# The second product of attention takes both operands in two parts for the first two pairs of heads too

## The chip, the cores and the metric

One core of a Trainium2 chip runs the whole program in one launch. The engines that matter are TensorE (PE in the profile; PEld is its weight load), VectorE (DVE), ScalarE (ACT), GpSimd (POOL) and SyncE (SP), whose queue issues every DMA. Each engine works through its own instructions in a fixed order. The metric is device microseconds of one execution, and three runs of the kernel before are given.

## The reference

Three blocks are chained, all in float32. Only the first is touched by the change; the other two follow it in the same program.

```python
def _attn_ref(q, k, v, g_q, g_k):          # q, k, v: (4, 12, 448, 64)
    q_n, k_n = rmsnorm(q, g_q), rmsnorm(k, g_k)
    scores = scale * q_n @ k_n^T
    attn = exp(scores - max) ; attn = attn / (sum + 1e-9)
    return attn @ v                          # the second product
...
x = attn_out as (1792, 768)
h = ((x @ w1) * (x @ w2)) @ w3 @ w_out      # first block of weights, d_ff 1024
g = h2 * clip(h2 + 3, 0, 6) / 6, h2 = h @ w_in ; out = g @ w_out2   # second, d_ff 2048
```

## The kernel before, in words

**Work and stages.** The 48 heads are taken as 24 pairs (index `i`), both heads of a pair at once. A pair is eight *steps* of scores: `score` (lines 627 and 628, two matmuls), `scale_max` on VectorE (634), `expo` on ScalarE (646). Eight steps later the same pair's probabilities come back through TensorE: `trans` (653) transposes them in seven blocks `kb` of 128 keys, four small matmuls each, into a PSUM bank of the tag "t", of which there are two. `thi` (662, ScalarE) copies a block from the bank to SBUF as `xh`. One step on, `tlo` (672, VectorE) would subtract it from the bank to give the rest, `xl`. Two steps on, `pv` multiplies the block with `v`. Blocks 0 to 2 and 4 to 6 belong to one head each; block 3 holds 64 keys of either head, and its two products run on separate halves of the array.

**Two forms of the second product.** `full(i)` is true for pairs 0 and 1. There `v` is loaded straight into `vo`, `xh` is plain float32, there is no `xl`, and a block's product is one float32 matmul (line 701, and line 687 for block 3), which the hardware runs as two instructions. For all other pairs `v` is loaded into `vr`, of which there is one buffer, and `vsplit` makes two parts of it: ScalarE rounds it (615), GpSimd subtracts (616). The parts stand side by side as 128 columns. A block then takes two matmuls in the reduced format float32r, one for `xh` (705, or 693 in block 3) and one for `xl` (706, or 693 again). Both leave two halves of the result in 128 rows of PSUM, so `xcopy` (713) moves one half and `xadd` (721, VectorE) adds the other.

**What runs between.** A stream of matmuls that doesn't depend on attention fills TensorE: first `wprime` (line 252, plain float32, 128 products, w3 times w_out), later layers 1 and 2. Their weights come from HBM as 64-bit numbers into four `raw` buffers and are converted by ScalarE (148, 149) and VectorE (151). `fill` hands out a fixed amount of this stream to every step. `at(t, ...)` and `SHIFT` put the small tasks into steps. A scheduler with its own model of time then orders the instructions of each engine. In the instruction stream of the first two pairs and what runs beside them, all of this is mixed closely.

```python
def full(i):
    return i in FULL                                  # 471
...
hi = ap.tile([P, S], F32 if full(i) else F32R, tag="xh", bufs=3, name="xh")   # 655
...
if full(i):                                           # 700
    nc.tensor.matmul(T["pv", i, j][:64, :S], vo[:, j, kb % 4], hi, ...)
    return
w = vo[:, j, kb % 4].rearrange("p a d -> p (a d)")
nc.tensor.matmul(ps, w, hi, start=(kb == 0), stop=False)
nc.tensor.matmul(ps, w, lo, start=False, stop=(kb == 6))
```

Of the kernel before, what the change touches and what calls it, by code (L numbers as in the profile page):

```python
# [36 lines left out]
NH = DM // 2  # L37
XB = 7
TAGS = ("s", "t", "v", "f")
FULL = (0, 1)  # L40
LG = 8
AHEAD = 3
K3 = 12
# [7 lines left out]
def fused_kernel(ctx: ExitStack, tc: tile.TileContext, nat, qT, kT, vin, gq, gk,  # L51
# [418 lines left out]
    def attention(ap, rate):  # L470
        def full(i):
            return i in FULL

# [945 lines left out]
```

## Time and profile before

| | |
|---|---|
| median of 3 runs | 1149.24 us (1142.69, 1149.24, 1151.27) |
| the profiled execution | 1141.81 us, span of its instructions 1140.0 us |
| TensorE busy | 1103.1 us, 97% of the span |
| weight loads | 944.0 us, 83% |
| VectorE, ScalarE, GpSimd busy | 850.8 (75%), 812.4 (71%), 177.9 (16%) us |
| DMA | 299.04 MB, 262 GB/s on average |

Averages hide that the stages differ: attention with `wprime` beside it fills roughly the first 190 us, attention with the next layers runs on to about 620 us, and the rest is matrix products alone. The plain float32 products of pairs 0 and 1 stand between 41.9 and 94.7 us. A busy TensorE isn't a TensorE at its peak, because the ends of pipelined matmuls are modelled; the distance from one start to the next is the better measure of what a matmul costs in a dense stretch.

### The profile page before, as it was taken

How to read it: one execution, taken by the hardware profiler on the slowest of the kernel's cores; microseconds unless marked ns; L12 is line 12 of the kernel's file. 1: busy time of each engine (PE TensorE's matmuls, PEld its weight loads, DVE VectorE, ACT ScalarE, POOL GpSimd, SP SyncE). 2: the span in 40 equal slices, each digit the busy share in tenths (PEclk: the TensorE clock that was granted, in tenths of full speed). 3: DMA queues.
4: the chain of work that ended last, by engine and by line, in shares of the span. 5: the costliest groups of instructions: out<-in, count | busy, mean ns of one | idle time of the engine just before them, and what ended most of it. 6: DMA issues, size and time to landing. Idle time of an engine off the chain costs nothing.

```text
span 1140.0 us, 17361 instructions
## 1 busy us (share of the span) xinstructions
PE 1103.1 (97%) x5483; PEld 944.0 (83%) x5483; DVE 850.8 (75%) x1927; ACT 812.4 (71%) x1729; POOL 177.9 (16%) x156
## 2 busy tenths in 40 slices
PE   5999999999999999999999999999999999999998
PEld 3545666788887888888888899899989989999998
DVE  5757988779866888778753225999988998887764
ACT  6989778899758878787754433766666776666764
POOL 1133223554322213221102000000000000000000
PEclk9999999999999999999999999999999999999999
DMA  8999655689889988997789998665469955434972
GB/s 267 331 317 342 213 171 164 243 293 377 272 279 316 308 295 269 336 342 253 232 287 324 382 362 299 217 214 200 164 228 362 389 172 168 153 117 160 335 264 74
DMA packets 109660, 299.04 MB, mean 262 GB/s; under 512 B 13280, under 2 KB 46048, under 8 KB 109568
## 3 DMA queue, kind: packets, MB, share of 16 engines
q1 hardware_dynamic: 109568, 297.93, 76.2%
q8 instruction: 43, 0.70, 0.3%
q14 instruction: 49, 0.40, 0.1%
HBM read 230.61 MB, written 67.27 MB: 261 GB/s over the span
## 4 chain that ended last, share of the span: by engine, by line
PE 60%; ACT 7%; DMA 7%; DVE 3%; issue 2%; POOL 0%; SPq 0%; ACTq 0%; POOLq 0%; DVEq 0%
PE acc L1304 17%; PE bank L391 10%; PE sB L1242 8%; PE sA L1242 8%; PE bank L396 5%; DMA rsb<-rsd 2%; PE bank L653 2%; ACT PP L646 1%; PE bank L88 1%; PE bank L89 1%; PE bank L90 1%; PE bank L627 1%; PE bank L628 1%; PE bank L706 1%; DMA raw<-in_wo_dram 1%
## 5 line engine op out<-in xcount | busy, mean ns | idle before, releaser
L1304 PE MATMUL acc<-g,wt 128*128 128x448 f32 x1008 | 211.7, 366 | 1.2 <-ACT g L1192 1.0
L1304 PEld LDWEIGHTS acc<-g,wt 128*128 128x128 f32 x1008 | 188.9, 188 | 17.7 <-ACT g L1192 1.9
L391 PE MATMUL bank<-xhl,ws 128*128 128x448 f32 x768 | 180.5, 367 | 1.6 <-ACT bs L367 1.3
L391 PEld LDWEIGHTS bank<-xhl,ws 128*128 128x128 f32 x768 | 143.5, 188 | 15.1 <-ACT bs L367 1.8
L634 DVE CUSTOM_DVE_ANT_0 PP<-bank,rb,rq 112x448 f32<-112x448 f32 x192 | 128.7, 675 | 27.4 <-PE bank L628 21.1
L646 ACT ACTIVATE PP<-PP,mx 112x448 f32<-112x448 f32 x192 | 127.5, 665 | 28.1 <-DVE mx L641 24.3
L1242 PE MATMUL sA<-xo,wt 128*128 128x448 f32 x504 | 112.0, 366 | 1.1 <-ACT u L1253 1.1
L1242 PE MATMUL sB<-xo,wt 128*128 128x448 f32 x504 | 112.2, 367 | 0.8 <-ACT u L1253 0.6
L252 PE MATMUL bank<-woh,w 128*128 128x384 f32 x256 | 97.6, 509 | 14.6 <-DVE woh L151 10.9
L1242 PEld LDWEIGHTS sB<-xo,wt 128*128 128x128 f32 x504 | 94.4, 188 | 9.9 <-ACT u L1253 1.9
L1242 PEld LDWEIGHTS sA<-xo,wt 128*128 128x128 f32 x504 | 94.6, 188 | 9.6 <-ACT u L1253 1.5
L662 ACT ACTIVATE xh<-bank 128x448 fp32r<-128x448 f32 (+1 forms) x156 | 83.1, 539 | 24.6 <-PE bank L653 20.5
L653 PEld LDWEIGHTS bank<-ident,PP 112*128 112x128 f32 x672 | 78.8, 141 | 23.9 <-issue 6.1
L1011 DVE TENSOR_TENSOR wt<-wf,wt 128x384 fp32r<-128x384 f32 x160 | 87.3, 555 | 15.1 <-ACT wt L1010 14.9
L672 DVE TENSOR_TENSOR xl<-bank,xh 128x448 fp32r<-128x448 f32 x142 | 87.4, 617 | 11.5 <-ACT xh L662 10.1
L653 PE MATMUL bank<-ident,PP 112*128 112x112 f32 x672 | 94.1, 261 | 1.5 <-DVE xl L672 1.1
L396 PE MATMUL bank<-xhl,ws 128*128 128x448 f32 x384 | 94.5, 366 | 0.0
L252 PEld LDWEIGHTS bank<-woh,w 128*128 128x128 f32 x256 | 48.9, 196 | 43.7 <-DVE woh L151 13.4
L148 ACT ACTIVATE raw<-raw 128x384 f32<-128x384 f32 (+1 forms) x112 | 63.8, 569 | 28.6 <-DMA raw<-in_wo_dram 11.6
L1010 ACT ACTIVATE wt<-wf 128x384 fp32r<-128x384 f32 x160 | 80.4, 517 | 4.8 <-PE acc L1304 2.7
L151 DVE SCALAR_TENSOR_TENSOR raw<-raw 128x384 int32<-128x384 int32 x80 | 48.9, 613 | 46.0 <-ACT raw L149 38.8
L627 PE MATMUL bank<-K,Q 128*112 128x448 f32 x192 | 77.7, 407 | 1.5 <-DVE mx L634 1.4
(134 smaller groups left out, 2110.3 us busy)
## 6 DMA issues: line engine op xcount, KB each, us to landing
ws<-w12d SPq DMA_DIRECT2D x48, 768.0 KB, 6.2
ws<-wpd SPq DMA_DIRECT2D x32, 768.0 KB, 6.5
wf<-wfd SPq DMA_DIRECT2D x56, 384.0 KB, 5.6
raw<-in_wo_dram SPq DMA_DIRECT2D x44, 384.0 KB, 5.8
td<-G SPq DMA_DIRECT2D x32, 448.0 KB, 2.5
G<-td SPq DMA_DIRECT2D x32, 448.0 KB, 6.2
raw<-in_w_dram SPq DMA_DIRECT2D x32, 384.0 KB, 6.9
w12d<-ws SPq DMA_DIRECT2D x16, 768.0 KB, 5.9
```

The lines of the kernel that those rows point to most:

```text
L252: nc.tensor.matmul(ps[:, :NH], W["w3"][a, c // 4][:, cs], W["woh"][c, n], start=c == 0, stop=c == M1 - 1)
L391: nc.tensor.matmul(ps[:, :S], w[:, 0, ks], x[:, y, :], start=k == 0 and y == 0, stop=False)
L396: nc.tensor.matmul(ps[:, :S], w[:, 1, ks], L["xhl"][i][:, 0, :], start=False, stop=k == KD - 1)
L627: nc.tensor.matmul(ps[:CP, :S], qs, k1[:, j, :], start=True, stop=False)
L634: anchors[8 * i + s].append(nc.vector.tensor_tensor_reduce(out=T["PP", i][:, c, sl], in0=ps[:CP, :S], in1=T["rb", i][:, sl], op0=ALU.mult, ...
L646: anchors[8 * i + s].append(nc.scalar.activation(v, v, AF.Exp, bias=T["m", i][:, 8 + s : 9 + s], accum_out=T["sum", i][:, s : s + 1]))
L653: nc.tensor.transpose(ps[:, c * CP : c * CP + CP], src[:, c, kb * P : kb * P + P], ident[:CP, :CP])
L662: nc.scalar.activation(hi, ps, AF.Copy)
L672: nc.vector.tensor_sub(lo, ps, hi)
L1011: nc.vector.tensor_sub(t[:, 1, :], src, t[:, 0, :])
L1242: mm = nc.tensor.matmul(ps[:, :S], w[:, a, ks], x[:, c, :], start=first and k == 0 and n == 0, stop=k == KD // 2 - 1 and n == 2, skip_grou ...
L1304: nc.tensor.matmul(ps, w[:, y, ns], x[:, z, :], start=first and a == 0, stop=end and a == 2, skip_group_check=h in "674")
```

## The change

The tuple of pairs that take the plain float32 form becomes empty. Pairs 0 and 1 then go through `vsplit`, `tlo`, the two reduced-format matmuls a block and `xadd`, as the other 22 pairs do.

```diff
-FULL = (0, 1)
+FULL = ()
```

Counted over the program: 12 matmuls of line 701 and 4 of line 687 go; 12 of line 705, 12 of line 706 and 8 of line 693 come. VectorE gets 14 subtractions of line 672 and 4 additions of line 721, ScalarE 2 copies of line 615, GpSimd 2 subtractions of line 616. The number of DMAs is the same; two loads of `v` go to `vr` and not to `vo`.

The scheduler orders the instructions anew. On TensorE the two orders are alike up to the 66th matmul and again for the last 3,706 of some 5,330. The first place is TensorE's order where the first block of pair 0 meets `v` (`K,Q`: scores, `ident,PP`: transposes, `xh,vo` and `xl,vo`: second product, `woh,w`: the `wprime` stream). Before:

```order
L653 MATMUL bank<-ident,PP 128x112 x4
L701 MATMUL bank<-xh,vo 64x448
L627 MATMUL bank<-K,Q 112x448
L628 MATMUL bank<-K,Q 112x448
L653 MATMUL bank<-ident,PP 128x112 x4
L701 MATMUL bank<-xh,vo 64x448
```

and now:

```order
L653 MATMUL bank<-ident,PP 128x112 x8
L627 MATMUL bank<-K,Q 112x448
L628 MATMUL bank<-K,Q 112x448
L252 MATMUL bank<-woh,w_107 128x384 x4
L705 MATMUL bank<-xh,vo 128x448
L706 MATMUL bank<-xl,vo 128x448
L705 MATMUL bank<-xh,vo 128x448
L706 MATMUL bank<-xl,vo 128x448
```

Both first blocks are now transposed before any product; two more scores stand ahead of the transposes, and four matmuls of the other stream stand between them and the first product.

The second place is SP's order of DMAs at the loads of `v` for the first pairs (`raw`: weights, `qr`, `kr`, `rb`: operands of later pairs). Before:

```order
L99 DMA nat<-in_nat_dram 112x1024
L99 DMA vo<-in_v_dram 128x512 x2
L99 DMA rb<-rkd 112x896
L99 DMA qr<-in_qT_dram 128x896
L99 DMA kr<-in_kT_dram 128x896
L99 DMA vr<-in_v_dram 128x512
```

and now, from the same DMA on:

```order
L99 DMA nat<-in_nat_dram 112x1024
L99 DMA vr<-in_v_dram 128x512
L99 DMA rb<-rkd 112x896
L99 DMA qr<-in_qT_dram 128x896
L99 DMA kr<-in_kT_dram 128x896
L99 DMA raw<-in_wo_dram 128x768 x3
L99 DMA wpd<-wst 128x256
L99 DMA raw<-in_wo_dram 128x768
L99 DMA wpd<-wst 128x256 x5
L99 DMA vr<-in_v_dram 128x512
L99 DMA qr<-in_qT_dram 128x896
L99 DMA raw<-in_w3t_dram 128x1024
```

One load of `v` stands ahead of the weights where three stood. The second now waits until GpSimd has split the first, because `vr` has one buffer, and a load of w3 stands behind it.

## Rows read from the trace of the kernel before

**Rows 1.** The page: busy tenths in 40 slices of 28.5 us.
```profile
PE   5999999999999999999999999999999999999998
PEclk9999999999999999999999999999999999999999
```

**Rows 2.** Busy time by stretch; the last three columns are granted clock, DMA share, GB/s.
```profile
core 0: us, PE busy (x) PEld busy (x) DVE busy (x) ACT busy (x) POOL busy (x), PEclk, DMA share, GB/s
40.00:60.00 20.00, 19.33 (x75) 10.58 (x75) 13.14 (x41) 20.00 (x45) 4.20 (x4) 1.00 1.04 332
60.00:80.00 20.00, 18.50 (x67) 9.78 (x66) 9.99 (x24) 15.29 (x34) 4.56 (x5) 1.00 1.01 319
80.00:100.00 20.00, 20.00 (x79) 10.92 (x78) 12.70 (x39) 19.12 (x42) 7.36 (x7) 1.00 0.98 345
100.00:120.00 20.00, 18.70 (x84) 12.62 (x83) 16.53 (x40) 19.56 (x45) 7.63 (x7) 1.00 0.93 321
120.00:140.00 20.00, 19.12 (x89) 12.57 (x88) 18.97 (x52) 15.36 (x36) 5.66 (x5) 1.00 0.69 216
...
620.00:1140.00 520.00, 512.21 (x2508) 469.81 (x2506) 385.14 (x722) 317.15 (x638) 2.29 (x2) 1.00 0.67 238
```

**Rows 3.** What PE waited for, 40 to 100 us: in total, times, longest.
```profile
PE bank L252 <- DVE wst L245: 1.5, 1, 1.5
PE bank L701 <- DMA vo<-in_v_dram: 0.5, 1, 0.5
```

**Rows 4.** The same, 100 to 140 us.
```profile
PE bank L705 <- ACT xh L662: 1.3, 1, 1.3
PE bank L706 <- DVE mx L641: 0.6, 1, 0.6
PE bank L653 <- DVE xl L672: 0.2, 1, 0.2
```

**Rows 5.** PE in order of time: start, us, line, count; plain float32 products and followers.
```profile
43.78 0.97 PE L701 MATMUL bank<-xh,vo 128*64 128x448 f32 x2
44.67 0.46 PE L627 MATMUL bank<-K,Q 128*112 128x448 f32 x1
44.97 0.37 PE L628 MATMUL bank<-K,Q 128*112 128x448 f32 x1
45.17 5.32 PE L252 MATMUL bank<-woh,w 128*128 128x384 f32 x16
...
53.08 0.97 PE L687 MATMUL bank<-xh,vo 64*64 64x448 f32 x4
53.98 0.46 PE L627 MATMUL bank<-K,Q 128*112 128x448 f32 x1
```

**Rows 6.** The same, products in two parts of pairs 2 and 3, and followers.
```profile
102.60 0.45 PE L706 MATMUL bank<-xl,vo 128*128 128x448 f32 x1
102.89 0.36 PE L705 MATMUL bank<-xh,vo 128*128 128x448 f32 x1
103.09 0.55 PE L653 MATMUL bank<-ident,PP 112*128 112x112 f32 x4
...
107.91 0.47 PE L705 MATMUL bank<-xh,vo 128*128 128x448 f32 x1 [1.30 <-ACT xh L662]
108.22 0.37 PE L627 MATMUL bank<-K,Q 128*112 128x448 f32 x1
...
115.67 0.66 PE L705 MATMUL bank<-xh,vo 128*128 128x448 f32 x1
116.17 0.55 PE L653 MATMUL bank<-ident,PP 112*128 112x112 f32 x4
...
133.31 0.47 PE L693 MATMUL bank<-xh,vo 64*128 64x448 f32 x2
133.72 0.46 PE L627 MATMUL bank<-K,Q 128*112 128x448 f32 x1
...
135.99 0.47 PE L693 MATMUL bank<-xl,vo 64*128 64x448 f32 x2
136.39 0.47 PE L705 MATMUL bank<-xh,vo 128*128 128x448 f32 x1
```

**Rows 7.** Instructions on tiles vr and xl: ns min/median/max, first and last start.
```profile
L615 ACT ACTIVATE vo<-vr x2: 622/630/637, 69.8 to 98.4; 128x512 fp32r<-128x512 f32 x2
L616 POOL TENSOR_TENSOR vo<-vr,vo x2: 1276/1401/1526, 70.9 to 99.1; 128x512 fp32r<-128x512 f32 x2
...
L672 DVE TENSOR_TENSOR xl<-bank,xh x13: 574/616/625, 101.1 to 137.1; 128x448 fp32r<-128x448 f32 x13
```

**Rows 8.** ACT by line, 40 to 100 us: busy, mean ns, idle before.
```profile
L148 ACT ACTIVATE raw<-raw 128x384 f32<-128x384 f32 x13 | 7.5, 580 | 3.7 <-DMA raw<-in_w_dram 3.7
L148 ACT ACTIVATE raw<-raw 128x512 f32<-128x512 f32 x8 | 5.4, 680 | 1.2 <-DMA raw<-in_w3t_dram 1.2
```

**Rows 9.** DVE by line, 38 to 140 us.
```profile
L721 DVE TENSOR_TENSOR xs<-bank,xs 64x448 f32<-64x448 f32 x3 | 1.8, 613 | 0.0
```

**Rows 10.** SP's own waits, 30 to 140 us.
```profile
SPq L99 <- POOL vo L616: 2.5, 2, 2.2
```

**Rows 11.** All matmuls of line 252: ns min/median/max, first and last start in us.
```profile
L252 PE MATMUL bank<-woh,w x256: 483/486/1010, 8.3 to 190.1; 128*128 128x384 f32 x128
```

## The prediction

> **What bounds the kernel now.** I read first the page's slices: from the second one on TensorE is busy at nine tenths or more and its clock is granted in full [rows 1]. Then the table by stretch. It says that from 40 to 100 us, where pairs 0 and 1 have their second product, nearly everything is full at once: TensorE 57.8 of 60 us, ScalarE 54.4, the DMA engines a share of 0.98 to 1.04; only VectorE (35.8) and GpSimd (16.1) have room [rows 2]. After 620 us TensorE is busy 512 of 520 us, so what is gained or lost early is carried to the end: nothing later absorbs it. Third, who kept TensorE waiting: 2.0 us in those 60 us, one wait for an eviction of `wprime` and one for the load of `v` [rows 3]. So TensorE sets the pace there, ScalarE and DMA are just behind it, and a saving on TensorE counts as long as these two keep up. In the next 40 us, where pairs 2 and 3 already go in two parts, TensorE waited 2.1 us [rows 4].
>
> **TensorE, removed.** In a dense stretch a plain float32 product lasts until the next start: 43.78 to 44.67, 0.89 us, and the two products of block 3, which run side by side, 53.08 to 53.98, 0.90 us together [rows 5]. Pairs 0 and 1 have six of the first and one of the second each: 12 x 0.89 + 2 x 0.90 = 12.5 us.
>
> **TensorE, added.** A matmul of a part takes 0.20 us to the next start (102.89 to 103.09), 0.29 to 0.31 (102.60 to 102.89, 107.91 to 108.22), or 0.50 behind a `wprime` matmul whose tail it carries (115.67 to 116.17). Block 3 takes 0.41 for both high parts and 0.40 for both low ones [rows 6]. I take 0.30, the middle of the three, since the new order has all three kinds of neighbours: 24 x 0.30 + 2 x 0.81 = 8.8 us. Saving 3.7 us. With 0.20 throughout it is 6.1; with 0.50 throughout there would be a loss of 1.1. The Trainium skill, "FP8 and Floating Point Precision", TensorE Precision Notes, says that true float32 takes four passes of the array. Two parts are two passes, so by that rule half of the array's time goes: with 0.20 us a pass, as in the shortest row, 14 slots x 0.4 = 5.6 us, and the forecast below would be 1142.7 instead of 1144.6. The rows have the removed side near that rule (0.89 against 0.80), but the added matmuls mostly cost more than a bare pass, so I stay with 3.7.
>
> **VectorE.** 14 subtractions of 0.616 us and 4 additions of 0.613 [rows 7, 9]: 11.1 us, of which 35.8 + 11.1 = 46.9 still fit into 60. The throughput costs nothing; the cover is VectorE's idle 24 us. But each subtraction stands between the copy `xh` and the second matmul of its block, and holds a "t" bank 0.62 us longer than before, so it can become a wait of TensorE. What such waits cost is seen where pairs 2 and 3 have 13 of these subtractions: 2.1 us in all [rows 4, 7]. For 14: 2.3 us. Bounds: nothing, if the new order covers every one; 14 x 0.616 = 8.6 us if every one lies bare. I take 2.3, because it is measured with the same neighbours and an equally full ScalarE (19.56 of 20 [rows 2]).
>
> **ScalarE and GpSimd.** Two more `vsplit`: 2 x 0.63 = 1.3 us on ScalarE, 2 x 1.4 = 2.8 on GpSimd [rows 7]. GpSimd has 44 us of room. ScalarE has none from 40 to 60 (20.00 of 20.00), and 4.7 us from 60 to 80 [rows 2], idle there because it waited for weights [rows 8]. Queued behind the first `vsplit` are the exponentials and the conversions. I cost it at nothing beyond the 2.3, since that stretch, too, had a copy of line 615 just ahead of it, at 98.4 [rows 7]; without the cover it is 1.3.
>
> **The first product and the loads.** Before, TensorE waited 0.5 us for the load of `v` at 41.9 [rows 3]. Now the two copies come behind the same load: 0.63 + 1.4 = 2.0 us later. The order puts in front of that product two more scores (0.5 us each by 44.67 to 45.17) and four `wprime` products, which are eight instructions, half of the sixteen that take about 5 us: 1.0 + 2.6 = 3.6 us [rows 5]. So the delay is covered; uncovered it would be 2.0. On SP's queue one load of `v` instead of three stands ahead of the weights. That is kind to a full DMA stretch. But the second and third load of `vr` now wait for GpSimd, and loads of w3 stand behind them. Such waits took 2.5 us for two [rows 10]. Two more, 2.5 us, are mostly hidden, as transfers issued earlier are still running at a share of 1.0 [rows 2]; I cost them at nothing, 2.5 if the DMA engines ran dry.
>
> **Sum.** -3.7 + 2.3 = -1.4 us. The profiled execution would go from 1141.81 to 1140.4 us (span 1140.0 to 1138.6). It stands 7.4 us below the median of the three runs, as low as the lowest of them. The four executions together have their middle at (1142.69 + 1149.24) / 2 = 1146.0, and I put the forecast on that: 1144.6, rounded 1145 us, which is 4.6 us below the median shown, though only 1.4 of it is the change. Chance 0.5 for a net of about -3 to 0.
>
> **Rival: the parts come late, slower.** The place is pairs 0 and 1, the price the subtractions. ScalarE is full there, so the copies `xh` come late, `xl` later still, and TensorE stands in order behind line 706 or behind a transpose that lacks a bank. Fully bare: -3.7 + 8.6 + 1.3 = +6.2, 1152.2 us. It decides from 3.7 / 14 = 0.26 us bare for each block on. For it: ScalarE 20.00 of 20.00; a wait of 1.3 us for one `xh` in the stretch in two parts [rows 4]. Against it: that stretch shows 0.16 us a block, and the scheduler put other work between. Chance 0.18.
>
> **Rival: the saving is hidden.** DMA share 1.0 says that the weights set the pace of `wprime`, whose matmuls stand in TensorE's fixed order; then a shorter product only becomes a wait for weights: 1146.0. For it: ScalarE's 4.9 us of waits for weights [rows 8]. Against it: TensorE itself waited for none of that [rows 3]. Chance 0.12.
>
> **Rival: ScalarE sets the pace.** Then its added 1.3 us are the whole effect, +1.3, 1147.3 us. For it the full 20 us at the start; against it the idle 4.7 us right after [rows 2]. The Trainium skill, "Perfetto Trace Analysis", Identifying the Most-Contended Engine, judges ScalarE by its busy share and TensorE by its weight loads, and would have ScalarE improved first; weight loads fill 10.58 of the same 20 us. By that rule this change loads the wrong engine. The waits show TensorE as the one that stops for almost nothing, so I give it 0.08.
>
> **Rival: all of it is kept.** Every wait is covered and the short spacing holds: -3.7 to -6.1, 1139.9 to 1142.3. Chance 0.12. That the change doesn't do what it says is excluded by the order: no plain float32 second product is left.
>
> **How the numbers follow.** The range is 1138 to 1154: from the largest saving (1139.9) and the late parts (1152.2), each moved outward by about 2 us, as runs of one kernel lie 8.6 us apart. A measurement tells about 1% from no change, 11.5 us, here below 1137.7 or above 1160.7. No case reaches either by itself. Faster by that needs the largest saving and low draws: 0.05. Slower needs the late parts and a stall of several us on top, since the order is new for some 1,600 matmuls: 0.07. Same: 0.88.
>
> **What would show it.** Second products of pairs 0 and 1 with starts 0.2 to 0.3 us apart; between 40 and 100 us fewer TensorE instructions of line 701's length, VectorE busy about 47 us, TensorE's waits near 4 us, naming `xh`, `xl` or `mx`; the last `wprime` matmul (190.1 us at its start before [rows 11]) about 1.4 us earlier, and everything behind it shifted by as much. Wrong would be waits of TensorE above 6 us there (late parts), waits for `woh` or `w` (weights), a first product later than about 46 us (the loads), or a difference that arises only after 400 us.

## The result and the profile after

The change makes the kernel slower: 1155.09 us (median of 21 runs, 1145.57 to 1162.66) against 1145.86 us (21 runs of the kernel before, 1138.68 to 1153.41), a ratio of 1.0083, 95% interval 1.0062 to 1.0103. By that ratio the change costs 9.5 us (the two medians lie 9.2 us apart), where 1.4 us of gain were forecast. The profiled execution has a span of 1154.2 us (1140.0 before).

The page of the changed kernel, TensorE and its granted clock in 40 slices, answers to [rows 1]:

```profile
PE   5998999999999999999999999999999999999998
PEclk9889999999999999999999999999999999999999
```

Two slices, 29 to 87 us, no longer have the full clock. The table by stretch, with the columns of [rows 2], says it finer:

```profile
40.00:60.00 20.00, 19.65 (x68) 12.48 (x67) 15.72 (x44) 19.78 (x45) 5.21 (x4) 0.83 1.02 319
60.00:80.00 20.00, 17.45 (x60) 10.33 (x61) 14.21 (x34) 12.09 (x24) 5.36 (x5) 0.83 0.92 319
80.00:100.00 20.00, 16.66 (x68) 10.33 (x66) 14.08 (x31) 19.43 (x45) 7.02 (x6) 1.00 0.88 287
100.00:120.00 20.00, 19.15 (x81) 13.53 (x82) 18.18 (x47) 18.37 (x41) 5.36 (x5) 0.91 0.99 316
120.00:140.00 20.00, 17.24 (x72) 11.38 (x71) 16.11 (x43) 15.71 (x37) 6.14 (x5) 0.91 0.66 218
...
41.00:47.00 6.00, 5.65 (x17) 3.85 (x17) 6.00 (x18) 5.78 (x14) 1.28 (x1) 0.50 1.00 303
65.00:71.00 6.00, 5.63 (x11) 2.59 (x10) 5.87 (x14) 4.77 (x10) 1.60 (x2) 0.50 0.79 242
102.00:105.00 3.00, 3.00 (x12) 2.36 (x12) 2.98 (x7) 2.63 (x6) 1.02 (x1) 0.50 1.02 356
126.00:129.00 3.00, 2.99 (x9) 2.18 (x10) 2.66 (x7) 1.81 (x4) 0.00 (x0) 0.50 1.02 375
```

The last four lines are cut to the places of the loss: a mean of 0.83 is some 7 us at 0.50, 1.2 GHz, and the rest at 2.4. Between 40 and 140 us TensorE ran at the lower level for about 20 us. Second, it is idle more: 90.2 us busy of these 100 instead of 95.7, although a matmul at 1.2 GHz stays busy longer. Third, ScalarE, full in the neighbouring stretches, has only 12.1 us of work from 60 to 80 (15.3 before). What TensorE waited for, first 40 to 100 us, then 100 to 140 us, answers to [rows 3, 4]:

```profile
PE bank L627 <- DVE mx L634: 3.1, 3, 2.2
PE bank L705 <- ACT xh L662: 1.5, 1, 1.5
PE bank L653 <- DVE xl L672: 1.1, 1, 1.1
PE bank L252 <- DVE mx L641: 0.3, 1, 0.3
...
PE bank L705 <- ACT xh L662: 3.7, 2, 2.6
PE bank L653 <- DVE xl L672: 0.4, 2, 0.2
PE bank L627 <- DVE mx L634: 0.2, 1, 0.2
```

10.3 us against 4.1. The longest waits are for the scores' reduction (`mx`) and for `xh`; the new `xl` accounts for 1.5 us. One can be followed to its source. The chain of waits of the changed kernel, 52 to 68 us (start, duration, what):

```profile
53.19 8.74 DMA raw<-in_w_dram
...
62.01 0.55 ACT raw L148
62.55 0.44 ACT raw L149
...
63.70 0.67 DVE PP L634
```

and VectorE and TensorE in order of time there:

```profile
63.01 0.77 DVE L151 SCALAR_TENSOR_TENSOR raw<-raw 128x384 int32<-128x384 int32 x1 [1.96 <-ACT raw L149]
63.70 0.67 DVE L634 CUSTOM_DVE_ANT_0 PP<-bank,rb,rq 112x448 f32<-112x448 f32 x1
```

```profile
61.80 0.45 PE L706 MATMUL bank<-xl,vo 128*128 128x448 f32 x1
64.44 0.72 PE L627 MATMUL bank<-K,Q 128*112 128x448 f32 x1 [2.19 <-DVE mx L634]
64.95 0.57 PE L628 MATMUL bank<-K,Q 128*112 128x448 f32 x1
...
67.64 7.17 PE L252 MATMUL bank<-woh,w 128*128 128x384 f32 x16 [0.26 <-DVE mx L641]
74.35 0.66 PE L627 MATMUL bank<-K,Q 128*112 128x448 f32 x1
```

A piece of weights arrives at 62.0. ScalarE converts it, VectorE finishes it, and the reduction of a score, which has nothing to do with it, stands behind it in VectorE's order. TensorE waits 2.2 us, its clock falls right after that, and the next sixteen `wprime` matmuls take 6.7 us to the next start (67.64 to 74.35) where the same sixteen took 4.9 before (45.17 [rows 5] to 50.04). Here one wait is paid twice. The follower of the sixteen in the kernel before:

```profile
50.04 0.66 PE L627 MATMUL bank<-K,Q 128*112 128x448 f32 x1
```

The last `wprime` matmul starts 8.0 us later than in [rows 11]:

```profile
L252 PE MATMUL bank<-woh,w x256: 483/486/1009, 8.1 to 198.1; 128*128 128x384 f32 x128
```

### The profile page after: what moved, and what is told of

The parts are those of the page before. It is cut to its first block, busy times and chain, and to the rows that moved or that the text cites. A ratio compares the mean times of both kernels' runs of the same rounds, so it can differ in the third digit from the quotient of the medians.

```text
span 1154.2 us, 17391 instructions
## 1 busy us (share of the span) xinstructions
PE 1109.1 (96%) x5483; PEld 952.6 (83%) x5483; DVE 867.3 (75%) x1945; ACT 814.4 (71%) x1731; POOL 179.3 (16%) x158
## 4 chain that ended last, share of the span: by engine, by line
PE 69%; DMA 14%; ACT 9%; DVE 4%; issue 2%; POOL 1%; SPq 0%; ACTq 0%; POOLq 0%; DVEq 0%
PE acc L1304 17%; PE bank L391 10%; PE sB L1242 8%; PE sA L1242 8%; PE bank L396 5%; PE bank L252 3%; PE bank L653 3%; DMA raw<-in_wo_dram 2%; PE bank L627 2%; PE bank L628 2%; PE bank L88 2%; PE bank L90 2%; PE bank L89 2%; DMA raw<-in_w_dram 2%; ACT PP L646 2%
## 5 line engine op out<-in xcount | busy, mean ns | idle before, releaser
L391 PE MATMUL bank<-xhl,ws 128*128 128x448 f32 x768 | 182.5, 370 | 2.0 <-ACT bs L367 1.2
L391 PEld LDWEIGHTS bank<-xhl,ws 128*128 128x128 f32 x768 | 145.3, 190 | 15.8 <-ACT bs L367 1.5
L252 PE MATMUL bank<-woh,w 128*128 128x384 f32 x256 | 100.7, 523 | 13.5 <-DVE woh L151 11.0
L672 DVE TENSOR_TENSOR xl<-bank,xh 128x448 fp32r<-128x448 f32 x156 | 96.0, 617 | 15.6 <-ACT xh L662 14.2
L662 ACT ACTIVATE xh<-bank 128x448 fp32r<-128x448 f32 x156 | 83.0, 537 | 30.1 <-PE bank L653 28.4
L396 PE MATMUL bank<-xhl,ws 128*128 128x448 f32 x384 | 95.6, 368 | 0.0
L148 ACT ACTIVATE raw<-raw 128x384 f32<-128x384 f32 (+1 forms) x112 | 63.7, 569 | 32.1 <-DMA raw<-in_wo_dram 12.8
L252 PEld LDWEIGHTS bank<-woh,w 128*128 128x128 f32 x256 | 51.5, 205 | 41.7 <-DVE woh L151 13.5
L396 PEld LDWEIGHTS bank<-xhl,ws 128*128 128x128 f32 x384 | 72.2, 189 | 6.9 <-issue 0.4
```

What stands on the lines that cost most here:

```text
L252: nc.tensor.matmul(ps[:, :NH], W["w3"][a, c // 4][:, cs], W["woh"][c, n], start=c == 0, stop=c == M1 - 1)
L391: nc.tensor.matmul(ps[:, :S], w[:, 0, ks], x[:, y, :], start=k == 0 and y == 0, stop=False)
L396: nc.tensor.matmul(ps[:, :S], w[:, 1, ks], L["xhl"][i][:, 0, :], start=False, stop=k == KD - 1)
L662: nc.scalar.activation(hi, ps, AF.Copy)
L672: nc.vector.tensor_sub(lo, ps, hi)
```

## The experiments

Three theories stood against each other: the clock (TensorE idles more, so it is granted less), the late parts (waits for what the two parts add), and luck of the order (any new order of the first 400 us moves the time by several us). Ratios are to the kernel before in the same session, with 95% intervals. *Idle* is what TensorE wasn't busy from 40 to 140 us, *clock* its mean granted clock there, *last* the start of the last `wprime` matmul. The last three come from one profile each, so a difference in them smaller than that between the two profiles of the same kernel says nothing.

| kernel | ratio | idle, us | clock | last, us |
|---|---|---|---|---|
| before; profiled again (e11) | 1 | 4.3; 4.2 | 1.00; 0.98 | 190.1; 191.4 |
| the change; profiled again (e12) | 1.0083 | 9.9; 11.7 | 0.90; 0.91 | 198.1; 198.6 |
| e1, pair 0 in two parts | 1.0066 (1.0040 to 1.0092) | 12.8 | 0.91 | 201.1 |
| e2, pair 1 in two parts | 1.0021 (0.9995 to 1.0048) | 7.4 | 0.95 | 192.8 |
| e3, pairs 0 to 3 plain | 1.0038 (1.0018 to 1.0058) | 2.6 | 0.97 | 196.9 |
| e4, one useless matmul a score | 1.0057 (1.0036 to 1.0078) | 9.6 | 0.95 | 197.0 |
| e16, two of them | 1.0072 (1.0041 to 1.0102) | 9.1 | 0.95 | 198.5 |
| e7, v of pair 1 early | 1.0069 (1.0044 to 1.0094) | 10.3 | 0.90 | 197.9 |
| e8, high part alone | 1.0042 (1.0018 to 1.0066) | 13.8 | 0.91 | 195.7 |
| e5, plain, written order | 1.0207 (1.0180 to 1.0233) | 9.5 | 0.95 | 203.4 |
| e6, parts, written order | 1.0243 (1.0216 to 1.0269) | 12.7 | 0.91 | 206.1 |
| e9, plain, lighter conversion | 0.9951 (0.9923 to 0.9980) | 0.7 | 0.98 | 187.7 |
| e10, parts, lighter conversion | 0.9935 (0.9910 to 0.9960) | 3.9 | 0.97 | 183.5 |
| e13, plain, pieces later | 1.0051 (1.0021 to 1.0081) | 5.4 | 0.95 | 196.3 |
| e14, parts, pieces later | 1.0076 (1.0045 to 1.0107) | 11.3 | 0.95 | 197.8 |
| e15, parts, copies on GpSimd | 1.0148 (1.0109 to 1.0187) | 11.4 | 0.86 | 202.7 |

**Profiled again.** No edit.

> The kernel before, profiled a second time. If the stretches at 1.2 GHz belong to the change, at most one between 38 and 140 us here (none in the first profile). If they come by chance, two or more, about as many as the change had (four, 20.5 us in all).

> The change, profiled a second time. If the stretches at 1.2 GHz belong to the change, again three or more between 38 and 140 us, 15 to 25 us in all, behind the same waits of TensorE. If they come by chance, none to one.

The second profiles repeat the first: the kernel before has 0.98 from 40 to 140 us, one short stretch at 1.2 GHz, the change 0.91, and the waits and the shift at the end of `wprime` come back (8.0 and 7.2 us). The stretches near 63, 101 and 125 us return, the one near 40 does not. So the falls behind the waits belong to the change; the one near 40 comes and goes: the second profile of the kernel before, e2 and e3 have it too.

**One pair at a time, and two more.**

```diff
-FULL = ()
+FULL = (1,)          # e1;  e2: (0,);  e3: (0, 1, 2, 3)
```

> Pair 0 alone takes its second product in two parts, pair 1 stays plain float32. Three theories of the 9 us that the change costs. Clock: without the plain products TensorE is idle in a larger share of the time between its waits, its granted clock falls to 1.2 GHz in some stretches, and these cost most of it (in the profile of the change four stretches before 130 us, about 20 us long, some 10 us of excess). It expects a stretch near 40 us to stay, those behind the products of pair 1 to be rarer, and 1.003 to 1.005 of the time before. Late parts: the waits for xh, xl and the scores' reductions are the loss; it expects half of the effect too, 1.003 to 1.005, but with the clock in full. Luck of the order: any new order of the first 400 us shifts the time by several us either way; it expects no relation to the number of pairs.

> Pair 1 alone takes its second product in two parts, pair 0 stays plain float32, so the first products stand where they stood. Clock: no fall near 40 us; falls only behind 60 us; 1.002 to 1.005. Late parts: waits for xh and xl of pair 1 alone, 1.003 to 1.005 with the clock in full. Luck of the order: anything from 0.995 to 1.01.

> The opposite direction: pairs 0 to 3 are plain float32. Added TensorE work is about 4 to 6 us (two pairs, 1.9 to 3.1 each), VectorE loses 18 operations. Clock: the clock in full over the first 130 us, so the added work shows, 1.000 to 1.005. Late parts: the waits of 2.1 us between 100 and 140 us go and the added work shows, 1.002 to 1.004. Luck of the order: anything from 0.995 to 1.01.

Pair 0 carries most of the loss (1.0066), pair 1 hardly any that is clear of 1 (1.0021); together they add up to about the loss of the change. Halves of one effect they are not: e1 lies above the 1.003 to 1.005 of both theories, e2 at the lower end of what the clock expected and below what the late parts did, though its interval reaches into both. That e2 would keep its full clock near 40 us was wrong, it is low there from 43.5 us. e1 waits for `xh` up to 97, 101 and 125 us, when the products of pair 0 are past (the last at about 77 us), so the parts themselves don't make these waits; that the order and the backlog behind the parts make them is argued, not shown. e3 shows the bound in the other direction: TensorE's waits are the shortest of all versions that leave nothing out (idle 2.6 us), and its added plain work then shows at the end of `wprime`, at 196.9 instead of 190.1 and 191.4. Its clock was not in full, as the clock theory expected, but 0.83 from 40 to 60 us.

**Work that nothing needs.** In `score`, for steps 6 to 25 once (e4), for 6 to 29 twice (e16):

```diff
+            for _ in range(2 if 6 <= 8 * i + s < 30 else 0):      # e16
+                nc.tensor.matmul(ps[:CP, :S], qs, k1[:, j, :], start=True, stop=True)
             nc.tensor.matmul(ps[:CP, :S], qs, k1[:, j, :], start=True, stop=False)
```

> The change as it is, and in 20 steps (6 to 25) the first score matmul is issued once more ahead of itself, into the same bank, which the second overwrites: 20 x 0.2 us of work that nothing needs, 4 us. Clock: TensorE is as busy again as before, most stretches at 1.2 GHz between 40 and 130 us go; 8 us less 7 to 10 us of excess plus 4 us of work, 1.000 to 1.005 of the time before, less than the change alone (1.008). Late parts: the waits stay and the work comes on top, 1.008 to 1.012. Luck of the order: anything.

> The change, with the first score matmul issued three times in steps 6 to 29, the first two overwritten: 48 x 0.2 us, 9.6 us of work that nothing needs. If TensorE only waits for others in this stretch, the work fits into what it lost to waits and to 1.2 GHz: 1.006 to 1.010, no more than the change alone. If TensorE sets the pace, the work comes on top: 1.013 to 1.018.

e4 lies between what the clock and the late parts expected. In e16 48 more matmuls, about 9.6 us, cost nothing that can be seen: e16's last `wprime` matmul starts at 198.5 us, the change's at 198.1 and 198.6. From 40 to 120 us e16 and the change read:

```profile
40.00:120.00 80.00, 74.10 (x313) 48.94 (x311) 61.19 (x147) 68.94 (x150) 25.01 (x21) 1.00 0.95 315
```

```profile
40.00:120.00 80.00, 72.92 (x274) 46.68 (x274) 62.19 (x154) 69.67 (x153) 22.95 (x20) 0.89 0.95 310
```

With more to do TensorE keeps 2.4 GHz in this stretch, does 39 more matmuls, and is as far on with the rest: by 120 us 34 scores have started in both. So the work fits into what the change lost to waits and to 1.2 GHz, as the first expectation said, and the full clock alone doesn't win the time. The waits hardly shrink, though: 9.1 us idle from 40 to 140 against 9.9 and 11.7. The larger part is paid by the clock, 0.95 there against 0.90 and 0.91, some 4 to 5 us of full-speed work (from 120 to 140 us e16 falls to 0.74, and the second profile of the change has 0.94 from 40 to 120). So e16 shows room for useless work; it doesn't exclude that TensorE set the pace and the clock it got back paid for most of that work.

**v of pair 1 early.** Its raw `v` goes into two buffers of the tag `xs`:

```diff
+            if i == 1:
+                T["vr", i] = [ap.tile([P, S], F32, tag="xs", bufs=8, name="vr1")[:, : 4 * D] for _ in range(2)]
...
```

> The change, but the raw v of pair 1 goes into two buffers of its own (of the results that aren't needed yet), so its load need not wait until GpSimd has split pair 0, and no load of weights stands behind that wait on SP's queue. Weights late through the loads of v: the waits for xh and for the scores' reductions between 60 and 130 us shrink, and 1.000 to 1.004 of the time before. Late parts or clock without the loads: as the change, 1.007 to 1.010. Luck of the order: anything from 0.995 to 1.01.

1.0069, the last `wprime` matmul at 197.9: the loads of `v` behind GpSimd's split are not the main cause; the interval leaves room for a small part. The edit also splits the rounding and the subtraction of this pair's `v` in two each.

**High part alone.** For pairs 0 and 1 `tlo` and the matmuls of `xl` are left out, and with them the low part of the probabilities.

```diff
-            if full(i):
+            if full(i) or i < 2:
                 return
...
```

> The change, with the low part of the probabilities left out for pairs 0 and 1: no subtraction on VectorE, half the matmuls. Late parts: without the 14 subtractions and 16 of 32 matmuls the loss goes, 0.993 to 1.000 of the time before. Clock: TensorE has even less to do between its waits, stretches at 1.2 GHz remain, 1.003 to 1.008. Luck of the order: anything.

Relieving TensorE and VectorE further undoes about half of the loss, 1.0042 against 1.0083, and not all of it. TensorE runs ahead and then stands:

```profile
79.52 0.37 PE L628 MATMUL bank<-K,Q 128*112 128x448 f32 x1
86.62 1.01 PE L653 MATMUL bank<-ident,PP 112*128 112x112 f32 x4 [6.73 <-ACT xh L662]
```

Late subtractions can't be the whole: there are none for these pairs, VectorE has 69.5 us of work from 40 to 140 us instead of 78.3, and TensorE has more idle time (13.8 us) than in the change. On ScalarE the copy `xh` of this wait stood behind a conversion that had waited 2.3 us for its weights, and behind six exponentials. Whether the half that went is the price of the subtractions or of the 16 matmuls (about 4.8 us at 0.30) this run can't tell.

**The written order.** Both kernels without the scheduler:

```diff
-    with _tile.TileContext(nc, schedule_with_timeline_sim=True) as tc:
+    with _tile.TileContext(nc, schedule_with_timeline_sim=False) as tc:
```

> The kernel before without the scheduler: every engine takes its instructions in the order in which the program writes them. The baseline for the next run; by itself it should be slower than before, by 1 to 10%.

> The change without the scheduler, to be compared with the run just before it. Luck of the order: with an order that is alike but for the operations themselves, the saving on TensorE shows, 0 to 6 us faster than the plain form in the written order. Clock and late parts as a property of the change itself: slower than it by 4 us or more, with more stretches at 1.2 GHz.

1168.08 against 1172.46 us, six runs each, 1165.80 to 1170.52 and 1170.39 to 1174.85: the two parts cost 4.4 us here too. So about half of the loss returns in a different order of the whole program, and the change is no gain there either. The two orders wait in different places, so this doesn't say how much of the 9.5 us belongs to the order that the scheduler chose.

**A lighter conversion.** In `convert`, for w3 and w_out alone, ScalarE's second operation is left out:

```diff
...
+        if light:
+            yield 0.7
+            nc.vector.tensor_scalar(w, hi, 3, None, op0=ALU.logical_shift_left)
+            yield 0.9
+            return
         nc.scalar.activation(lo, top, AF.Copy, scale=2.0 ** -13, bias=2.0 ** -14 - 0.5)
...
```

> The kernel before with a lighter conversion of the weights of w3 and w_out: ScalarE's second operation on each (line 149) is left out, and with it the three lowest bits of these weights; about 32 operations of 0.6 us, 19 us of ScalarE, less before 120 us. ScalarE sets the pace of the first 120 us: faster than before by 4 us or more. TensorE sets it: 0.998 to 1.000. It is the baseline of the next run.

> The change with the same lighter conversion (the three lowest bits of w3 and w_out left out). Saving hidden by ScalarE: with ScalarE relieved, the products in two parts show their saving of about 3 us a pair, 2 to 6 us faster than the run just before this one, no wait of TensorE for xh above 1 us between 60 and 130 us, and fewer stretches at 1.2 GHz. Late parts or clock as a property of the two parts alone: slower than the run just before it by 4 us or more, as without the lighter conversion. Luck of the order: anything.

Both are faster than the kernel before, and the loss is gone: 1138.56 and 1139.27 us, the intervals of the two ratios overlap. The last `wprime` matmuls, e9 first:

```profile
L257 PE MATMUL bank<-woh,w x256: 482/486/1009, 7.5 to 187.7; 128*128 128x384 f32 x128
```

```profile
L257 PE MATMUL bank<-woh,w x256: 482/486/1008, 7.3 to 183.5; 128*128 128x384 f32 x128
```

Up to there the change now saves 4.2 us instead of losing 8. Half of the expectation failed: nothing of the 4.2 is left at the end, and one wait for `xh` was 1.5 us. TensorE is busy less between 200 and 700 us (487.1 of these 500 us in e10, 491.4 in e9), but the two profiles of the kernel before already differ there by 2.9 us (489.9 and 487.0), so this may be scatter. These two are the versions that beat both kernels, at the price of three bits of two weight matrices. What they changed is not the pace of the weights: in all sixteen profiles of the scheduler's order, e9 and e10 too, ScalarE has begun 33 to 35 of the 42 conversions (line 148) by 100 us, whatever TensorE has to do. What is lighter is ScalarE's work beside it, one operation fewer for each of these pieces. The conversions begun by 100 us in the kernel before, the change and e10 (ScalarE's time in them, count, and the last three columns of [rows 2]):

```profile
0.00:100.00 100.00, 21.17 (x35) 1.00 0.96 311
0.00:100.00 100.00, 20.36 (x34) 0.93 0.91 296
0.00:100.00 100.00, 20.45 (x35) 0.98 0.95 316
```

**Pieces later, and copies on GpSimd.** e13 and e14 put the pieces of w1 and w2 only behind the last six pieces of w3 (first half of the diff); e15 gives their copy to GpSimd (second half):

```diff
         for a, h in halves:
-            order += [("a", a, h)] + ones[:1]
-            del ones[:1]
+            order += [("a", a, h)]
+            if a >= 5:
+                order += ones[:1]
+                del ones[:1]
...
-            nc.scalar.activation(t[:, 0, :], f, AF.Copy)
+            nc.gpsimd.tensor_copy(t[:, 0, :], f)
```

> The kernel before, with the ten pieces of the next layer's weights (w1, w2) that are converted beside w3 moved behind it: the first six pieces of w3 no longer have one after each. Nothing is left out; ScalarE and DMA have less to do between 60 and 110 us and more behind it. Weights and ScalarE set the pace there: faster than before, 0.994 to 0.999. TensorE sets it: 0.999 to 1.002. It is the baseline of the next run.

> The change with the same pieces moved behind. Saving hidden by weights and ScalarE: with these relieved, TensorE's waits between 60 and 130 us are below 6 us and the loss against the plain form (1.008 without the relief) goes to between 0.996 and 1.003 of the run just before it. Late parts or clock as a property of the two parts alone: again 1.005 or more of it.

> The change, with ScalarE's copy of the high part of these ten pieces (line 225, 10 x 0.55 us) given to GpSimd, which has room. The DMA is as it was, so this tells ScalarE's time from the arrival of the weights. ScalarE's time: part of the loss goes, 1.002 to 1.006 of the time before. Arrival of the weights: 1.007 to 1.010.

e13 contradicts its own idea: the plain form becomes slower, 1.0051. e14 stands 0.0025 above it with overlapping intervals, as expected for a hidden saving, but TensorE is idle for 6.4 us from 60 to 130 us and not below 6, and for 11.3 us from 40 to 140, so this pair supports little. e15 takes 5.5 us off ScalarE and is the slowest in the scheduler's order, above both expectations; ScalarE's work from 60 to 80 us is 11.8 us (12.1 in the change), and the clock the lowest of all (0.86). The copies are no slower on GpSimd (0.53 us against 0.55), so their length doesn't hold the `raw` buffers longer. This speaks against the time of these copies as the cause; why e15 is slower than the change stays open.

## Why the prediction was wrong

**"TensorE sets the pace there, ... and a saving on TensorE counts as long as these two keep up."** This step failed. The condition was named and not tested: ScalarE and DMA were "just behind", which was read as room. They didn't keep up: TensorE, relieved, waited 10.3 us instead of 4.1 from 40 to 140 us and spent about 20 us at 1.2 GHz. Added work still showed (e3, 196.9 instead of 190.1), work taken away didn't (the change and e8 are both slower than the kernel before). e16 shows room from one side (9.6 us of work at no visible cost), e8 a wait from the other (further ahead, then 6.7 us), and e10, with the conversions lighter, keeps 4.2 us up to the end of `wprime`. That the queues of ScalarE and VectorE around the conversions are what held TensorE is the reading that fits these runs and the wait followed above; e15, which relieves ScalarE and loses, keeps it from being shown.

**The saving of 3.7 us** was a fair size. In the changed kernel the products follow each other in 0.19 to 0.50 us, as assumed, and with the lighter conversions 4.2 us show at the end of `wprime`.

**"For 14: 2.3 us"** of new waits was mis-sized: TensorE's waits rose from 4.1 to 10.3 us between 40 and 140 us. They were priced from the waits beside 13 subtractions, and only 1.5 us of those that came name `xl`. The others were for reductions and copies that stood behind other work on VectorE and ScalarE: a conversion in the wait followed above, at 125 us two conversions and the operands of a later pair. The stretch they were priced from also had fewer weights to convert: 7 pieces from 100 to 140 us in the kernel before, against 14 from 60 to 100.

**The clock was missing from the sum.** It stood at full in [rows 1, 2] and was taken as given. About 20 us at half speed cost up to 10 us of full-speed work, more than any term that was priced. The parts add up in order: some 6 us of waits, up to 10 us of clock, less a saving of 4 to 6, against a shift of 8.0 us at the end of `wprime`. But e16 warns against calling the 10 us the cause: part of that time would have been waited for anyway.

**The rivals.** "The saving is hidden" (0.12) had the place, but not the path: from 40 to 140 us no wait of TensorE in the change names `woh` or `w`. Where late weights cost time, they did so through the other engines' queues, and the clock fell behind the wait; its price of zero left out both. "The parts come late" had the sign and the nearest price (+6.2), with a mechanism that e8 shows not to be the whole. The first product started at 48.9 us, later than the 46 us allowed, but behind two more scores, the transposes and eight `wprime` matmuls in a stretch at half speed; TensorE didn't wait for `v` there. The Trainium skill, "Perfetto Trace Analysis", Identifying the Most-Contended Engine, would have had ScalarE improved first; e9 did that and gained 0.5%, so this run agrees with the page more than the 0.08 did; e15, which also relieved ScalarE, lost. The price of that rival, ScalarE's added 1.3 us, is far below the 9.5 us measured.

**The carry to the median** used a middle of four executions (1146.0); 21 runs have 1145.86, so that step held.

What stays open: the split of the loss between the scheduler's order (e1 and e2 aren't halves, e13 moves the plain form by 0.5%), the queues of ScalarE and VectorE, and the parts themselves, and where e10 loses its 4.2 us. "Nothing later absorbs it" held only roughly: from the last `wprime` matmul to the end the profiles of the scheduler's order take 943 to 957 us, 949.9 and 953.6 in the kernel before, 956.1 and 952.1 in the change. A second buffer for `vr` and a version that shortens the loads of the weights weren't tried.

## What to carry to other kernels

When four resources are full in the same stretch, ask what happens to each after the change, and test for slack before pricing a saving: a few useless matmuls in the stretch tell whether it has room, if the clock is read beside the time. A wait of 2 us on TensorE can cost more than 2 us: in the change those of 2.2 and 2.6 us were followed by stretches at 1.2 GHz, where a score's two matmuls started 0.51 us apart instead of 0.30. It isn't so every time: e16 kept its full clock behind a wait of 2.1 us at 66 us. An operation's price on a busy in-order engine includes what is queued ahead of it, here a conversion that itself waits for a DMA.

## What the runs showed of the hardware

Where TensorE had few waits its clock stayed up: in the profiles with two plain pairs in the scheduler's order it was 0.95 to 1.00 from 40 to 140 us with 0.7 to 5.4 us idle, in the change 0.90 and 0.91 with 9.9 and 11.7. The format alone doesn't decide it: e10, in two parts throughout, had 0.97 with 3.9 us idle. 39 more matmuls from 40 to 120 us came with a clock of 1.00 over that stretch (e16), against 0.89 and 0.94 in the two profiles of the change. At 0.50 a score's second matmul starts 0.51 us behind the first (64.44 to 64.95), at full clock 0.30 (44.67 to 44.97 [rows 5]).

The Trainium skill, "TensorE: Matmul & The Clock Gate", Part 1, describes a clock that activity releases and idleness takes back, and advises to keep the array busy. The runs agree on both: the falls stand behind waits, and with e16's useless work the clock stayed full up to 120 us. They add that this need not save time: e16 is not measurably faster than the change.
